# Idle products ahead of the data: 24 of 512 columns in place of 96 of 128 columns

## The chip, the cores and the metric

The kernel runs on one core of one Trainium2 chip. The metric is the device time of one execution in microseconds (us). The median of five executions of the kernel before is 330.3 us; they lie at 329.09, 329.21, 330.30, 330.36 and 330.72.

The engines are named as the profile names them: PE is TensorE's products and PEld its weight loads, DVE is VectorE, ACT is ScalarE, POOL is GpSimd, and SP is SyncE, whose queue (SPq) issues the transfers.

## The reference

Two stages follow each other: a retention layer in its parallel form, and a gated feed-forward layer.

```python
# q, k, v: 8 batches, 8 heads, 576 positions, 64 numbers a head, fp32
scores = (1 / sqrt(64)) * q @ k.T
gamma  = 1 - 2.0 ** (-5 - arange(8))              # one decay a head
ret    = (scores * where(i >= j, gamma ** (i - j), 0)) @ v
x      = ret.transpose(0, 2, 1, 3).reshape(4608, 512)
out    = (sigmoid(x @ w_gate) * (x @ w_val)) @ w_out   # 512 -> 1536 -> 512
```

## The kernel before

**The work.** The decay is split: k is multiplied by a table of falling powers and q by one of rising powers, so what is left of the mask is a triangle. The positions are taken in chunks of 128. The first 768 rows of x are made in a special way, as three pairs of chunks (`PAIRS`): a pair's k and q are cast to bf16 and scaled (`cast_pair`, L270), turned by TensorE with products against an identity (`pair_t`, L310, called through `turn`), copied out of PSUM by ScalarE (L320), multiplied to scores (`pair_qk`, L329), masked by VectorE (L334) and multiplied by v (`pair_intra`, L416). A state, the sum of k times v over earlier chunks, is kept beside (`pair_st`, L348, and `pair_inter`, L426). The other rows follow in steps (`slot`, `slot_of_two`), placed between the products of the feed-forward layer: gate and value products (`h_half` L881, `h_both` L802, `h_units` L698), sigmoid on ScalarE, product with the gate on VectorE, and the output product (`op_first` L952, `op_units` L765).

**The order.** It is written out by hand: each engine runs its instructions in the order in which the program names them. TensorE is one queue in order, so an instruction that waits holds all behind it. SyncE issues nearly all loads, in order, into a pool of 18 buffers (`ld`); a load waits until the buffer that it takes has been read. The weights are cast from fp32 to bf16 by GpSimd, ScalarE and VectorE (L244, L249).

**The idle products.** At the start there is nothing for TensorE to do until the first k and q are loaded and scaled. `blank` is a tile of 128 x 128 zeros, set by VectorE (L170). `idle_bank` (L174) takes a tile of 128 x 128 fp32 from the PSUM pool `ffn`, whose three buffers are a bank (512 fp32 a partition) each. `fill(n)` (L179) issues 4n products of blank by blank into it. Nobody reads the result. `fill(10)` comes right after `blank`; then the first pairs are worked on with more of it between:

```python
    cast_pair("q", 0, 0, nc.vector)
    turn("k", 0, 0, *TR)
    turn("q", 0, 0, *PV)
    fill(3)
    cast_pair("q", 0, 1, nc.vector)
    pair_qk(0, 0, QK)
    turn("k", 0, 1, *TR)
    fill(2)
    turn("q", 0, 1, *PV)
    fill(3)
    ...
```

and so on with `fill(2)`, `fill(1)` and, after a second `idle_bank()`, `fill(3)`: 24 units, 96 products (L182) in all, each with its own weight load.

Of the kernel before, what the change touches and what calls it, by code (L numbers as in the profile page):

```python
# [9 lines left out]
FP32 = mybir.dt.float32  # L10
# [6 lines left out]
def kernel(  # L17
# [19 lines left out]
    nc = tc.nc  # L37
# [4 lines left out]
    P = 128  # L42
# [18 lines left out]
    ffn_psum = ctx.enter_context(tc.tile_pool(name="ffn_psum", bufs=3, space=PS))  # L61
# [107 lines left out]
    blank = consts.tile([P, P], BF16)  # L169
    nc.vector.memset(blank, 0.0)  # L170

    idle = []

    def idle_bank():  # L174
        idle.append(ffn_psum.tile([P, P], FP32, tag="ffn", name=f"idle_{len(idle)}"))

    idle_bank()

    def fill(n):  # L179

        for i in range(4 * n):
            nc.tensor.matmul(idle[-1], lhsT=blank, rhs=blank, start=True, stop=True)  # L182

    fill(10)
    def tables(shape, pattern, step, put, fix=None):

# [643 lines left out]
# [9 lines that stand above are left out]
# [8 lines left out]
    fill(1)  # L847
    turn("q", 1, 1)
    idle_bank()
    fill(3)  # L850
    pair_intra(0, 0, 0)
# [221 lines left out]
```

## Time and profile before

| what | value |
| --- | --- |
| median of five executions | 330.3 us |
| the profiled execution | 329.21 us, of which the span (first to last instruction) is 327.5 us |
| TensorE busy | 321.3 us (98%), 3696 products |
| VectorE, ScalarE, GpSimd busy | 148.6, 139.1, 104.1 us |
| idle products (L182) | 96, 8.6 us of busy time, 1.05 to 13.3 us of the span |
| first gate product of the feed-forward layer (hg, L881) | 17.39 us |
| last product's modelled end | about 324.2 us |

How to read it: the profile shows one execution. A product's length in it runs to its modelled end, and products overlap, so how fast TensorE goes is seen from the distance between starts. "Idle before" is the time in which an engine did nothing, with what ended it. The chain of waits goes back from the last instruction to what released it, step by step, and so names what is on the path to the end.

### The profile page before, as it was taken

To read this page: it belongs to the slowest core of one execution; us is meant where nothing else is said; L and a number is where in the kernel's file an instruction comes from. 1 tells how busy PE (TensorE), PEld (TensorE's weight loads), DVE (VectorE), ACT (ScalarE), POOL (GpSimd) and SP (SyncE) were. 2 spreads that over 40 slices of the span, in tenths; PEclk is the share of its full clock that TensorE was granted. 3 is DMA by queue.
4 is the path that set the end of the run, shared out by engine and by line. 5 is a ranking of instruction groups with operands and counts; after the bars stand their busy time and mean duration, and the time that the engine had idled before them with its cause. 6 is when DMAs were issued, how large, how long until landed. Compare 5 with 4: busy or idle time off the path is not lost.

```text
span 327.5 us, 8910 instructions
## 1 busy us (share of the span) xinstructions
PE 321.3 (98%) x3696; PEld 173.0 (53%) x3696; DVE 148.6 (45%) x335; ACT 139.1 (42%) x314; POOL 104.1 (32%) x138
## 2 busy tenths in 40 slices
PE   8899999999999999999999999999999999999996
PEld 8774557856546554455444544454445544544443
DVE  6945756656505463445334534344444433404410
ACT  6654545554524354324532543335334533343321
POOL 5784637454535463018300840075003000000000
PEclk9999999999999999999999999999999999999999
DMA  7999999999996999809890799069805820010003
GB/s 209 352 396 384 377 242 213 202 177 218 206 196 143 215 219 200 187 2 199 199 247 2 151 229 254 15 124 214 210 2 73 304 109 2 34 74 27 1 32 98
DMA packets 144794, 55.16 MB, mean 168 GB/s; under 512 B 125168, under 2 KB 136688, under 8 KB 144752
## 3 DMA queue, kind: packets, MB, share of 16 engines
q1 hardware_dynamic: 144608, 54.44, 68.3%
q8 instruction: 29, 0.48, 0.6%
q10 hardware_dynamic: 144, 0.13, 0.1%
q14 instruction: 13, 0.11, 0.1%
HBM read 37.75 MB, written 9.44 MB: 144 GB/s over the span
## 4 chain that ended last, share of the span: by engine, by line
PE 97%; ACT 1%; DVE 1%; issue 0%; ACTq 0%
PE h L698 50%; PE op L765 25%; PE op L952 3%; PE hg L802 3%; PE hv L802 3%; PE val L509 2%; PE idle L182 2%; PE row L483 1%; PE row L491 1%; PE val L525 1%; PE op L754 1%; PE qkp L329 1%; ACT qT L320 1%; PE hv L881 1%; PE hg L881 1%; PE kTp L310 0%
## 5 line engine op out<-in xcount | busy, mean ns | idle before, releaser
L726 DVE TENSOR_TENSOR gv<-g,h 128x512 bf16<-128x512 bf16 (+1 forms) x96 | 62.8, 654 | 103.3 <-PE h L698 100.5
L698 PE MATMUL h<-xT,wv_sb 128*128 128x512 bf16 (+2 forms) x432 | 100.7, 356 | 0.0
L698 PE MATMUL h<-xT,wg_sb 128*128 128x512 bf16 (+2 forms) x432 | 100.7, 355 | 0.0
L722 ACT ACTIVATE g<-h 128x512 bf16<-128x512 f32 (+1 forms) x96 | 54.7, 570 | 94.4 <-PE h L698 90.9
L765 PE MATMUL op<-wo_sb,gv 128*128 128x512 bf16 x372 | 84.0, 379 | 0.0
L698 PEld LDWEIGHTS <-wg_sb 128*128 128x128 bf16 x432 | 42.0, 98 | 41.2
L698 PEld LDWEIGHTS <-wv_sb 128*128 128x128 bf16 x432 | 41.9, 98 | 40.4
L765 PEld LDWEIGHTS <-gv 128*128 128x128 bf16 x372 | 35.3, 98 | 41.0
L288 POOL CAST v<-v 128x512 bf16<-128x512 f32 x29 | 17.7, 610 | 89.4 <-PE val L509 80.1
L283 POOL TENSOR_TENSOR qk<-k,ktab 128x512 bf16<-128x512 f32 x30 | 31.3, 1042 | 33.4 <-DMA k<-in_k_dram 21.7
L741 ACT COPY ob<-op 128x512 f32<-128x512 f32 x33 | 19.3, 585 | 35.7 <-PE op L765 34.8
L283 POOL TENSOR_TENSOR qk<-q,qtab 128x512 bf16<-128x512 f32 x28 | 29.5, 1055 | 1.3 <-DMA q<-in_q_dram 1.0
L498 DVE TENSOR_TENSOR pt<-row,tri 128x256 bf16<-128x256 f32 x60 | 21.6, 416 | 13.9 <-PE row L491 12.4
L567 ACT CAST xT<-val 128x256 bf16<-128x256 f32 x46 | 15.0, 380 | 22.9 <-PE val L525 21.4
L610 DVE TENSOR_TENSOR s<-s,row 128x256 f32<-128x256 f32 x39 | 16.2, 416 | 1.3
L459 ACT CAST sb<-s 128x256 bf16<-128x256 f32 x44 | 15.9, 421 | 0.3 <-DVE s L610 0.2
L553 DVE COPY glance<-val 128x1 f32<-128x1 f32 x24 | 2.7, 154 | 23.4 <-PE val L525 22.7
L952 PE MATMUL op<-wo_sb,gv 128*128 128x512 bf16 x48 | 11.7, 380 | 0.0
L509 PEld LDWEIGHTS <-v 64*64 64x64 bf16 x480 | 6.2, 108 | 7.5 <-issue 7.5
L525 PE MATMUL val<-T,sb 64*64 64x64 bf16 x368 | 9.7, 195 | 0.3 <-DVE glance L553 0.3
L809 DVE TENSOR_TENSOR gv<-g,hv 128x512 bf16<-128x512 bf16 x10 | 6.7, 683 | 7.0 <-PE hv L802 7.0
L182 PE MATMUL idle<-blank 128*128 128x128 bf16 x96 | 8.6, 259 | 1.1 <-DVE blank L170 1.1
(102 smaller groups left out, 241.6 us busy)
## 6 DMA issues: line engine op xcount, KB each, us to landing
out_dram<-ob SPq DMA_DIRECT2D x31, 256.0 KB, 3.1
k<-in_k_dram SPq DMA_DIRECT2D x26, 256.0 KB, 3.8
q<-in_q_dram SPq DMA_DIRECT2D x26, 256.0 KB, 4.1
v<-in_v_dram SPq DMA_DIRECT2D x26, 256.0 KB, 4.5
wg<-in_moe_w_gate_dram SPq DMA_DIRECT2D x12, 256.0 KB, 5.1
wv<-in_moe_w_val_dram SPq DMA_DIRECT2D x12, 256.0 KB, 5.1
wo<-in_moe_w_out_dram SPq DMA_DIRECT2D x12, 256.0 KB, 4.9
k32p<-in_k_dram SPq DMA_DIRECT2D x6, 256.0 KB, 5.2
```

The lines of the kernel that those rows point to most:

```text
L283: eng.tensor_tensor(out=natural_qk[s][:, i].rearrange("p m (y d) -> p y m d", y=2), in0=by_halves(loaded[s][1 - i]), in1=tab, op=ALU.mult)
L288: eng(out=natural["v", s], in_=loaded[s][2])
L459: eng(out=state[key], in_=src)
L498: nc.vector.tensor_tensor(out=probs[s][:, y], in0=row_ps[s][y][:, 0], in1=tri.unsqueeze(1).to_broadcast([P, M, 64]), op=ALU.mult)
L610: nc.vector.tensor_tensor(out=new, in0=running[b], in1=p, op=ALU.add)
L698: nc.tensor.matmul(out, lhsT=w_sb[:, kc, fc * P:(fc + 1) * P], rhs=xT[:, kc, t0 + a:t0 + e], start=(kc == 0), stop=(kc == NKC - 1))
L722: nc.scalar.activation(out=g[:, 0:n], in_=h1[:, 0:n], func=AF.Sigmoid)
L726: nc.vector.tensor_tensor(out=gvs[some[0]][:, a:e], in0=g[:, 0:n], in1=h2[:, 0:n], op=ALU.mult)
L741: (eng or on_act)(out=ob, in_=opp)
L765: nc.tensor.matmul(opp, lhsT=gvs[fc][:, nb * P:(nb + 1) * P], rhs=wo_sb[:, fc, :], start=(fc == 0), stop=(fc == NFC - 1))
L802: nc.tensor.matmul(ps, lhsT=(wg_sb if what == "g" else wv_sb)[:, kc, fc * P:(fc + 1) * P], rhs=xT[:, kc, 0:4 * P], start=(kc == 0), stop=( ...
L952: nc.tensor.matmul(opps[nb], lhsT=gvs[fc][:, nb * P:(nb + 1) * P], rhs=wo_sb[:, fc, :], start=(fc == 0), stop=(fc == NFC - 1))
```

## The change

Each four products of 128 columns become one of 512. The moving operand is the same 128 x 128 zeros, read four times over through a broadcast in the middle dimension; the idle tile becomes as large as the bank. The units and their places stay, so 24 products and 24 weight loads are left of 96 and 96.

```diff
     def idle_bank():
-        idle.append(ffn_psum.tile([P, P], FP32, tag="ffn", name=f"idle_{len(idle)}"))
+        idle.append(ffn_psum.tile([P, 4, P], FP32, tag="ffn", name=f"idle_{len(idle)}"))
 
     idle_bank()
 
     def fill(n):
 
-        for i in range(4 * n):
-            nc.tensor.matmul(idle[-1], lhsT=blank, rhs=blank, start=True, stop=True)
+        for i in range(n):
+            nc.tensor.matmul(idle[-1], lhsT=blank, rhs=blank.unsqueeze(1).to_broadcast([P, 4, P]), start=True, stop=True)
 
     fill(10)
```

The instruction lists of the two programs differ on TensorE in these products and weight loads alone. On SyncE the order of the loads is the same, but three neighbouring pairs trade the buffers that they take: w_val's second and third piece for columns 8 to 11, w_out's first two rows of blocks, and k and q of step 1.

## Prediction

> **What bounds the kernel now.** I read the page first, then TensorE's waits, then the timeline and the chain of waits of the first 14 us, because the change touches nothing later.
>
> From the page: span, busy time of the first engine, and the granted clock.
>
> ```profile
> span 327.5 us, 8910 instructions
> ...
> PE 321.3 (98%) x3696; PEld 173.0 (53%) x3696; DVE 148.6 (45%) x335; ACT 139.1 (42%) x314; POOL 104.1 (32%) x138
> ...
> PEclk9999999999999999999999999999999999999999
> ```
>
> The reader is to see that TensorE is busy for 321.3 of 327.5 us, and the chain that ended last is 97% PE. Of the rest, about 3.3 us lie behind the last product, when the result is stored.
>
> All that TensorE waited for (waiter, releaser: total us, times, longest us):
>
> ```profile
> PE idle L182 <- DVE blank L170: 1.1, 1, 1.1
> PE qkp L329 <- ACT qT L320: 0.7, 3, 0.3
> PE st L348 <- ACT sbd L358: 0.7, 1, 0.7
> ```
>
> The first three rows, 2.5 us, lie in the first 16 us. From 16 us to the end only 0.5 us of waiting is left. So after the start TensorE is a queue without gaps: a delay or a gain that reaches 17.4 us, where the first gate product (hg, L881) starts, goes through to the end one to one. Everything rests on the first 17 us.
>
> TensorE's timeline there (start, length, line, what, count, idle before):
>
> ```profile
> 1.05 4.45 PE L182 MATMUL idle<-blank 128*128 128x128 bf16 x40 [1.05 <-DVE blank L170]
> 5.29 0.63 PE L310 MATMUL kTp<-ident,kp 128*128 128x128 bf16 x4
> 5.72 0.60 PE L310 MATMUL qTp<-ident,qp 128*128 128x128 bf16 x4
> 6.14 0.85 PE L182 MATMUL idle<-blank 128*128 128x128 bf16 x12
> 7.24 0.42 PE L329 MATMUL qkp<-qT,kT 64*64 64x128 bf16 x16 [0.24 <-ACT qT L320]
> 7.58 0.40 PE L310 MATMUL kTp<-ident,kp 128*128 128x128 bf16 x4
> 7.82 0.61 PE L182 MATMUL idle<-blank 128*128 128x128 bf16 x8
> 8.27 0.39 PE L310 MATMUL qTp<-ident,qp 128*128 128x128 bf16 x4
> 8.49 0.83 PE L182 MATMUL idle<-blank 128*128 128x128 bf16 x12
> 9.47 0.42 PE L329 MATMUL qkp<-qT,kT 64*64 64x128 bf16 x16 [0.15 <-ACT qT L320]
> ```
>
> A length here runs from the first start to the last modelled end, so I take spacing from starts. The first 40 idle products take 5.29 - 1.05 = 4.24 us to the next start, 106 ns each. The last 12 (8.49, length 0.83, one product 0.219 long) give (0.83 - 0.219) / 11 = 56 ns. The array thus ran at half rate until about 6.2 us, although the row of the granted clock shows 9 everywhere; the spacing is what I trust. One product of 128 columns is 315 ns long in the slow part and 219 in the fast one.
>
> The chain of waits (start, share in us, what) shows which of the idle products are on the path:
>
> ```profile
> 1.05 4.45 PE idle L182 x40
> 5.50 0.44 PE kTp L310 x4
> ...
> 7.98 0.45 PE idle L182 x8
> 8.43 0.24 PE qTp L310 x4
> ...
> 11.95 0.33 PE idle L182 x4
> ...
> 12.65 0.67 PE idle L182 x12
> ```
>
> So 64 of the 96 are on it; the other 32 fill time in which TensorE would wait for ScalarE's copy of qT anyway.
>
> **The change, part by part.**
>
> *Products.* 96 products and 96 weight loads become 24 and 24: 144 fewer instructions on TensorE (8910 to 8766). The columns stay 12,288. The instruction lists of the two programs show no other instruction of TensorE moved and no wait of it added.
>
> *The first ten.* No row shows a product of 512 columns at half rate. At full rate L802 gives it: 8 of them take 1.73 us in the chain of waits, 216 ns each, against 56 for 128 columns, a factor of 3.86. Bounds at half rate: 3.86 x 106 = 409 ns and 4 x 107 = 428 ns. Ten take 4.09 to 4.28 us, against 4.24. I take 4.24, because a rate of 1.2 columns per ns (128 / 107) leaves no fixed part to save. Even the lower bound gains only 0.15 us. More cannot be had here: kp, the next thing TensorE needs, is ready at 4.89 (GpSimd, 3.85 + 1.04), and qp at 5.44 (VectorE, 4.51 + 0.93), while qTp starts at 5.72.
>
> *The other fourteen.* At full rate 4 x 56 = 224 ns become 216, 8 ns less. On the path are 2 + 1 + 3 of them: 6 x 8 = 0.05 us. The other eight end earlier by 0.06 us in all, and TensorE then waits that much longer for qT (0.24 and 0.15 us now). The operand is blank read four times over; no row has such an operand on TensorE. The nearest rows are L802 (216) and four separate reads (224), so the cost lies between 0 and -0.05.
>
> *The bank.* The idle tile grows from 512 bytes a partition to the whole bank, in a pool whose other tiles are whole banks already. No reader waits for it, and the later writers are on the same engine: nothing.
>
> *Loads.* The order of SyncE's queue stays, but three neighbouring pairs of loads trade buffers, and so waits: wv of rows 1 and 2 for columns 8 to 11, wo 0 and 1, and k and q of step 1. The largest wait on that queue between 20 and 60 us is 2.9 us. The last of that wv is cast at 33.51 and TensorE wants it at 35.41 (slack 1.9); wo 1 is cast at 33.84 and wanted at 39.30 (5.5); q of step 1 is cast at 52.62 and turned at 56.51 (3.9). For the last pair the worst is that k's issue, which ends at 43.22, waits as long as q's now does, to 44.93: 1.7 us against 3.9. Cost nothing; without that cover it would be up to the excess over the slack.
>
> *Sum.* 0 (-0.15 to +0.04) for the first ten, -0.05 for the rest: about -0.1 us. The profiled execution took 329.21 us (span 327.5 and 1.7 around it), so it would become 329.1. But it is among the lower of five executions (329.09 to 330.72); from their median, 330.3, the forecast is **330.2**. Of this kernel about 0.3%, 1.0 us, can be told from no change.
>
> **A rule weighed against these rows.** The rows say 56 and 216 ns. The Trainium skill, "TensorE: Matmul & The Clock Gate", section "Back-to-back issue gap", states for streams of weight loads and products about 81 ns a product at 128 columns and 131 at 512. By it, an estimate, the idle work would fall from 96 x 81 = 7.8 us to 24 x 131 = 3.1, so the fill would no longer span the wait for data; by the rows it stays within 0.3 us of what it was. The rows decide. The same page, section "What's actually happening", says that the clock is released by time and not by a number of products, in windows that run free of the kernel's start; that supports equal releases, but no single trace can show it.
>
> **The rivals.**
>
> *Slower: the clock is released later.* For it: 106 ns turned into 56 only after 5.1 us of work, and if what is watched includes weight loads, the change takes away three in four. Against it: at half rate both forms keep the columns streaming without a gap. Price: one pass, from the qkp at 7.24 to that at 9.47, has 1.25 us of TensorE work on the path (7.24 to 8.49), which would double; and the 12 idle products behind it, 0.67 us now, would take 1.28 and outlast ScalarE's copy by some 0.4. So a release one pass later costs up to 1.65 us, and a release half a pass later 0.8: 331.1 to 331.95. It decides if the idle products of the second fill, from 6.1 us on, and those of the third still start about 400 ns apart. I give it 0.20.
>
> *Slower: code or loads late.* The 29 instruction packets of queue q8 take 0.6% of 16 x 327.5 us, 1.1 us each; each now falls 144 instructions later in the work. One that TensorE had to wait for would cost about 1.1 us: 331.3. Against it: TensorE waits for none of the 29 now. With the loads above, 0.05.
>
> *Faster: the release comes sooner.* The five executions lie at 329.09 and 329.21 and then at 330.30 to 330.72. If the time of the release separates them and wide products bring it forward each time, the median becomes that of the lower ones, 329.1. For it: nothing in the trace but the spread. Against it: an earlier release alone is worth little, because qp of the second half (VectorE, 7.24 + 0.69 = 7.93, held by its load) lets qTp start at most 0.3 us before its 8.27. I give it 0.18.
>
> **How the numbers follow.** No change within 0.3%: 0.57; slower 0.20 + 0.05 = 0.25; faster 0.18. The range runs from the faster case, with its 329.1 inside, to most of the later release: 329.0 to 331.8. The likeliest case alone: 329.7 to 330.7.
>
> **What would show it.** TensorE's timeline after: ten wide products from 1.05, about 427 ns apart, and kTp at 5.2 to 5.35; the qkp rows within 0.1 us of 7.24 and 9.47; hg (L881) at about 17.4; from there the same spacing, 216 ns for each product of 512 columns. The forecast is wrong if the wide products start 216 ns apart early, if qkp moves by over 0.5 us, if TensorE gets a wait for issue, or if k of step 1 makes turn wait at 56.5.

## The result and the profile after

The changed kernel takes 330.21 us (median of 38 executions, 329.14 to 333.63), the kernel before 329.46 (66 executions, 328.95 to 330.72). The ratio is 1.003, with a 95% interval of 1.002 to 1.0039: **slower by 0.3%**, 0.75 us between the medians. The five executions that the prediction started from, with a median of 330.3, had by chance drawn the kernel before too high by 0.84 us.

The spread has changed more than the middle. Of the 38 executions six lie above 331.5, three of them at 333.3 to 333.6; of the 66 before none lies above 330.8.

The page of the changed kernel, and what its TensorE waited for (waiter, releaser: total us, times, longest):

```profile
span 328.1 us, 8766 instructions
...
q8 instruction: 28, 0.46, 0.6%
```

```profile
PE st L348 <- ACT sbd L358: 0.7, 1, 0.7
PE qkp L329 <- ACT qT L320: 0.5, 3, 0.2
PE st L348 <- issue: 0.4, 1, 0.4
...
PE kTp L310 <- POOL kp L270: 0.2, 1, 0.2
```

Two rows are new. One is a short wait for kp. The other is a stop of TensorE in L348 that nothing in the profile releases: "issue" means that the engine waited for no semaphore that is seen.

The timeline of TensorE after the change:

```profile
1.05 4.12 PE L182 MATMUL idle<-blank 128*128 128x512 bf16 x10 [1.05 <-DVE blank L170]
5.01 0.39 PE L310 MATMUL kTp<-ident,kp 128*128 128x128 bf16 x4
...
6.72 0.42 PE L329 MATMUL qkp<-qT,kT 64*64 64x128 bf16 x16 [0.17 <-ACT qT L320]
7.39 0.40 PE L310 MATMUL kTp<-ident,kp 128*128 128x128 bf16 x4 [0.25 <-POOL kp L270]
...
9.44 0.42 PE L329 MATMUL qkp<-qT,kT 64*64 64x128 bf16 x16 [0.18 <-ACT qT L320]
...
16.17 0.35 PE L348 MATMUL st<-vp,kp 64*64 64x64 bf16 x11
16.96 0.25 PE L348 MATMUL st<-vp,kp 64*64 64x64 bf16 x5 [0.44 <-issue]
...
17.81 0.61 PE L881 MATMUL hg<-xT,wg_sb 128*128 128x256 bf16 x4
```

The same sixteen products of L348 in the kernel before, in one piece:

```profile
16.35 0.44 PE L348 MATMUL st<-vp,kp 64*64 64x64 bf16 x16
```

The reader is to see three things. The wide products start as forecast, about 427 ns apart, but the array changed to its full rate sooner in this execution, so qkp starts 0.5 us earlier (6.72 against 7.24); most of that is given back in the wait for kp. At 16.2 us TensorE is still 0.2 us ahead. Then the sixteen products, which have no wait in their instructions, break after the eleventh. From the start of the eleventh to that of the twelfth 0.63 us pass, where there were 0.03, and hg comes at 17.81 instead of 17.39, 0.42 late. The two spans differ by 0.6 us; the last 0.14 gathers in small pieces after 100 us and was not followed.

**What stops it.** TensorE's code comes in packets of 16 KB on queue q8: 29 before, for 7392 products and weight loads, and 28 after, for 7248. That makes a packet about 256 instructions. I call the place where one packet's instructions end and the next one's begin a border. In the changed kernel's trace the stop stands between TensorE's 449th and 450th instruction. In the stretch before it, one such packet travels among the loads:

```profile
q1 hardware_dynamic: 758, 0.73, 104.5%
q8 instruction: 1, 0.02, 2.7%
```

That is the view of the transfers from 14 to 16 us: 16 engines fully taken by loads, and one code packet. The trace's transfer records have it from 14.71 to 15.59 us. TensorE stops at 16.32 and goes on at 16.96, 1.37 us after the packet's end. In the kernel before, that packet lands at 11.02, and TensorE reaches its 449th instruction at 13.98. The change took 144 instructions out ahead of this point, so the border moved to a later place in the work. There the packet has less time, for two reasons. It starts 3.0 us after TensorE has reached the border before (its 193rd instruction, at 11.69), where in the kernel before it starts 1.5 us after (8.60). And TensorE, with many short products, goes from the one border to the next in 4.6 us in place of 5.4.

### The profile page after: what moved, and what is told of

It is laid out like the page before. It is cut to its first block, busy times and chain, and to the rows that moved or that the text cites. A ratio compares the mean times of both kernels' runs of the same rounds, so it can differ in the third digit from the quotient of the medians.

```text
span 328.1 us, 8766 instructions
## 1 busy us (share of the span) xinstructions
PE 321.2 (98%) x3624; PEld 167.9 (51%) x3624; DVE 148.5 (45%) x335; ACT 139.2 (42%) x314; POOL 104.8 (32%) x138
## 3 DMA queue, kind: packets, MB, share of 16 engines
HBM read 37.75 MB, written 9.44 MB: 144 GB/s over the span
## 4 chain that ended last, share of the span: by engine, by line
PE 95%; DMA 1%; ACT 1%; DVE 1%; issue 0%; POOL 0%; SPq 0%; ACTq 0%
PE h L698 50%; PE op L765 25%; PE op L952 3%; PE hv L802 3%; PE hg L802 3%; PE val L509 2%; PE row L483 1%; PE row L491 1%; DMA k32p<-in_k_dram 1%; PE val L525 1%; PE op L754 1%; PE hv L881 1%; PE hg L881 1%; PE qkp L329 1%; PE st L348 1%; PE idle L182 0%
## 5 line engine op out<-in xcount | busy, mean ns | idle before, releaser
L610 DVE TENSOR_TENSOR s<-s,row 128x256 f32<-128x256 f32 x39 | 16.2, 416 | 1.3
L483 PE MATMUL row<-T 64*64 64x64 bf16 x480 | 9.7, 197 | 0.0
```

Of the source, the lines that this page charges most:

```text
L610: nc.vector.tensor_tensor(out=new, in0=running[b], in1=p, op=ALU.add)
```

## The experiments

Theory 1 is the one just given: the code is late, and only where the border lies matters. Theory 2 is the rival that I had held likelier: the width of the products, or the fewer weight loads, cost something through the clock or the array. All kernels compute the whole output.

For the reading of all of them: the interval of a ratio is 95%, and the kernel before took 329.41 us (35 executions) beside the first four and 329.29 (23 executions) beside the others.

**Narrow products, and more instructions.**

```diff
-    fill(10)
+    def fill_small(n, w):
+
+        for i in range(n):
+            nc.tensor.matmul(idle[-1][0:w, 0:w], lhsT=blank[:, 0:w], rhs=blank[:, 0:w], start=True, stop=True)
+
+    fill_small(96, 53)
```

> As the kernel before, but the first fill is 96 products of 53 columns in place of 40 of 128: the same 4.24 us, and 112 more instructions, where the change has 144 fewer. Code comes in packets of 256 instructions, so 112 more put the packet borders where 144 fewer put them. Theory 1 (code late): TensorE stops for 'issue' in st L348 at about 16.5 us, as after the change, 0.2 to 1 us; time 0.2 to 0.5% over before, with single executions above 331. Theory 2 (width: fewer weight loads or wide products cost, through the clock or the array): all products are narrow and weight loads are more than before, so no stop, and the time of before within 0.1%.

Measured: 330.14 us (329.08 to 332.27), ratio 1.0031 (1.0015 to 1.0048). The whole loss of the change is there with narrow products and more weight loads than before. The profile fell on the shortest execution, and even that shows the stop (this kernel's lines are 5 further on, so L348 is L353):

```profile
16.13 0.58 PE L353 MATMUL st<-vp,kp 64*64 64x64 bf16 x16
```

0.58 us in place of 0.44. The view of waits doesn't list this stop, because the modelled lengths of the products cover it; the starts show it. It stands behind the 705th instruction of TensorE: 449 + 256, the next border, at the same place in the work. The packet ended at 15.17, and TensorE went on at 16.46, 1.29 us later. Theory 2 fails here as the cause of the loss.

**Wide products, and as many instructions as before.** The later 14 units stay wide; the first fill is in small pieces.

```diff
-    fill(10)
...
+    fill_small(82, 62)
```

> As the changed kernel, with its 14 later wide products, but the first fill is 82 products of 62 columns (4.24 us), so that TensorE has as many instructions as before the change ahead of each real one. Theory 1 (code late): no stop for issue at 16.5 us, and the time of before or up to 0.2 us below it. Theory 2 (width of the later products): slower by 0.2 to 0.4%, as after the change.

Measured: 329.43 us (328.98 to 330.02), ratio 1.0001 (0.9989 to 1.0013), and no stop in L348. The fourteen wide products cost nothing that can be measured. As it has 82 products in its first fill, it doesn't speak for the ten wide ones there; the kernel of half width, further on, does for 256 columns.

This trace has a stop all the same, one border later, behind the 705th instruction, which here stands at the same place in the work as in the kernel before. The same eight products in the kernel before and here (L886 is L881, 5 lines further on):

```profile
19.41 1.04 PE L881 MATMUL hg<-xT,wg_sb 128*128 128x256 bf16 x8
```

```profile
19.49 1.18 PE L886 MATMUL hg<-xT,wg_sb 128*128 128x256 bf16 x8
```

Between the 705th and the 706th instruction 0.25 us pass, where there are 0.11 in the kernel before. The packet ended at 19.01, and TensorE went on at 20.40, 1.38 us later. So a border can be short of time in a kernel that hasn't fewer instructions, too; here it cost the traced execution 0.14 us.

**First fill narrow, the rest wide.** 84 instructions fewer.

```diff
-    fill(10)
+    def fill_narrow(n):
+
+        for i in range(4 * n):
+            nc.tensor.matmul(idle[-1][:, 0, :], lhsT=blank, rhs=blank, start=True, stop=True)
+
+    fill_narrow(10)
```

> The first fill as before (40 narrow products), the other 14 units wide: 84 instructions fewer than before. Theory 1 (code late): between two borders of 256 instructions TensorE needs 5.0 us there, against 3.9 us with 144 fewer and 5.3 before, so no stop or a rare one: within 0.1% of before. Theory 2 (fewer weight loads after the first fill): at least half of the change's 0.3%. If what matters is the number of instructions taken away, 84 of 144 of it, 0.17%.

Measured: 329.37 us (328.87 to 329.69), ratio 1.0001 (0.9992 to 1.0009), no stop. More than half of the 144 instructions are gone without a cost that can be measured.

**The changed kernel once more.**

> The changed kernel itself, beside the others on one chip, for a second trace. Theory 1 (code late): again a stop for issue at the eleventh to twelfth product of st L348 at 16.3 to 16.5 us; its length is what differs between executions, so the traced execution's time over 329.2 is about the stop less 0.2. Theory 2: the first difference to before lies elsewhere, at the release of the clock.

Measured: 330.06 us (329.38 to 332.01), ratio 1.0024 (1.0012 to 1.0035). The profiled execution took 330.06 us too, and has the stop at the same instruction, longer:

```profile
16.28 0.35 PE L348 MATMUL st<-vp,kp 64*64 64x64 bf16 x11
17.26 0.25 PE L348 MATMUL st<-vp,kp 64*64 64x64 bf16 x5 [0.63 <-issue]
```

0.82 us from start to start, against 0.63 in the first trace, and a span of 328.3 us against 328.1: the 0.2 us by which the two differ. The expectation, 329.2 plus the stop less 0.2, gives 329.8; it was 330.06.

**Half the width.** 48 products of 256 columns, 96 instructions fewer.

```diff
-        for i in range(n):
-            nc.tensor.matmul(idle[-1], lhsT=blank, rhs=blank.unsqueeze(1).to_broadcast([P, 4, P]), start=True, stop=True)
+        for i in range(2 * n):
+            nc.tensor.matmul(idle[-1][:, 0:2], lhsT=blank, rhs=blank.unsqueeze(1).to_broadcast([P, 2, P]), start=True, stop=True)
```

> 48 idle products of 256 columns: 96 instructions fewer than before, at the same length of time. Theory 1 (code late): on the undisturbed times of the kernel before, TensorE passes the 256 instructions ahead of the second border in 4.5 us, against 3.9 with 144 fewer and 5.0 with 84 fewer, so the stop is there only when the packet is late by more than usual: 0 to 0.15% over before, an occasional execution above 331, and where there is a stop, it is in front of the instruction 48 later than in the changed kernel. A theory by which each instruction taken away costs the same gives two thirds of the change, 0.2%.

Measured: 329.17 us (328.56 to 329.54), ratio 0.9983 (0.9962 to 1.0005), no stop in the trace and no execution above 329.6. The median lies a little below what theory 1 allowed (0 to 0.15% over before), the interval reaches into it, and there were no late executions at all. Two thirds of the 144 instructions are gone, and none of the loss is there; the 0.2% of a cost for each instruction taken away lies outside the interval. Here all idle products, those of the first fill too, are wider than before.

**The loads held back.** The changed kernel; SyncE stops behind its twelfth load until the first state is written, and the weights are loaded and cast later.

```diff
-    load_w(0, 2)
-    load_w(2, 2)
...
     tile_sv(0, 0, (on_act, on_act))
+    gate_sb = consts.tile([64, M, 64], BF16)
+    nc.sync.dma_start(out=gate_sb, in_=sbd[0][half(0), :, half(0)])
+    load_w(0, 2)
+    load_w(2, 2)
...
```

> The changed kernel, with SyncE's queue held after the first twelve loads until the first state is written (about 14.5 us); the weights come some 6 us later, so the time is above before by several us and says nothing. The question is the first code packet of TensorE. If it is late because it waits behind loads on the transfer engines, it starts at 12 to 13.5 us in place of 14.7 to 14.9, and TensorE doesn't stop in front of st L348's twelfth product (apart from waits for weights). If its delay has nothing to do with loads, it starts at 14.2 to 14.9 and the stop of 0.2 to 0.8 us stays.

Measured: one execution, 335.87 us, as it has to wait for its weights. The transfers from 12 to 16 us, in the changed kernel first and then in this one (stretch, length, busy time of the engines with counts, granted clock, DMA share, GB/s):

```profile
12.00:14.00 2.00, 2.00 (x68) 1.39 (x70) 1.49 (x3) 0.75 (x1) 1.80 (x4) 1.00 1.06 355
14.00:16.00 2.00, 1.33 (x56) 1.09 (x48) 1.93 (x4) 1.35 (x4) 1.85 (x4) 1.00 1.07 372
```

```profile
12.00:14.00 2.00, 2.00 (x67) 1.36 (x68) 1.49 (x3) 0.74 (x1) 1.67 (x4) 1.00 0.30 91
14.00:16.00 2.00, 1.33 (x57) 1.08 (x49) 1.92 (x4) 1.31 (x4) 0.39 (x1) 1.00 0.03 6
```

TensorE's part (the first number behind the length) is the same in both, and it reaches the border before, its 193rd instruction, at 11.72 here and at 11.69 there. What differs is the transfers, 1.06 of the engines' time against 0.30, and GpSimd, which has no weights to cast. The packet now starts at 13.06 us, where it started at 14.71 and 14.91, and L348 (L338 here) runs through:

```profile
16.21 0.44 PE L338 MATMUL st<-vp,kp 64*64 64x64 bf16 x16
```

So without the loads the packet came 1.7 to 1.9 us sooner, and the stop was gone. This is one execution, and when TensorE asks for a packet isn't recorded. The other packets of the nine traces agree, though. For each I take the time from TensorE's reaching the border before to the packet's start, and the share of the engines that the loads had taken in the 1.5 us ahead of that start. With the engines free (share under 0.05), none of 65 packets started later than 1.50 us. With them full (over 0.9), 58 of 145 did, up to 4.49 us. Late packets go with loads.

This kernel begins exactly as the changed one does, and shows by chance the other thing: its array was still at half rate in kTp (0.63 us for four, against 0.39 in the changed kernel's first trace), and its first fill took as long as that of the kernel before.

```profile
1.05 4.45 PE L172 MATMUL idle<-blank 128*128 128x512 bf16 x10 [1.05 <-DVE blank L160]
5.29 0.63 PE L300 MATMUL kTp<-ident,kp 128*128 128x128 bf16 x4
```

The moment at which the array changes its rate thus differs between executions that start alike, and in the nine traces it doesn't go with the width.

**The kernel before, without its second fill.** A try at a better one.

```diff
     turn("k", 0, 1, *TR)
-    fill(2)
     turn("q", 0, 1, *PV)
```

> The kernel before with narrow products, without the first fill(2) (8 products) ahead of the turning of q's second half, where the chain of waits has 0.45 us of it and the data are ready 0.3 us earlier; 16 instructions fewer. If those products are on the path: 0.2 to 0.3 us less than before (0.06 to 0.1%). If VectorE or the loads bound that pass: no difference. Theory 1 (code late): 256 instructions in 5.0 us there, so no stop.

Measured: 329.25 us (328.85 to 329.4), ratio 0.9981 (0.9959 to 1.0002); between the medians 0.04 us. In its trace the time goes into a wait:

```profile
8.23 0.40 PE L310 MATMUL qTp<-ident,qp 128*128 128x128 bf16 x4 [0.57 <-DVE qp L270]
```

TensorE waits for VectorE where it made idle products before, and qTp starts at 8.23 against 8.27. What the chain of waits had as 0.45 us of idle products was a cover over a wait for data. Neither this kernel nor the one of half width is faster than before by more than the measurement can tell.

**All traces together.** From the transfer records and the starts of TensorE's instructions: when the packet behind the border that matters (the second packet of the queue for the kernel with 112 more instructions, the first for the others) has landed, when TensorE reaches the border, and the stop. The stop is the distance between the two starts at the border; where there is none, it is 0.03 or less, and 0.11 in the row of the next border. Times in us.

```
kernel                    landed  border reached  between  stop
before                     11.02          13.98     2.96   none
changed                    15.59          16.32     0.73   0.63
changed, second trace      15.86          16.43     0.58   0.82
112 more, narrow           15.17          16.28     1.12   0.17
as many as before           9.02          14.06     5.04   none
  its next border          19.01          20.14     1.13   0.25
84 fewer                   13.11          15.60     2.49   none
96 fewer, half width       13.55          15.77     2.22   none
changed, loads held        13.93          16.36     2.43   none
16 fewer, no second fill   12.38          13.91     1.53   none
```

Where there was a stop, TensorE went on 1.29 to 1.40 us after the packet's end; where 1.53 us or more lay between, there was none. One rule covers all ten rows. At every other border of the nine traces 2.0 us or more lay between.

## Why the prediction was wrong

- **The first ten products.** Right in size. Behind the first, they start 426 to 427 ns apart until the array changes its rate. kTp started at 5.01 and not between 5.2 and 5.35, because the array changed its rate 1.4 us sooner than in the trace of before; the loads held gave 5.29.
- **The other fourteen.** Right: 215 to 216 ns apart. The 0.05 us is too little to be told in any time measured here. The read of the zeros through a broadcast has no price of its own: 216 ns is also what L802 takes.
- **The bank and the loads that trade buffers.** Right: no wait of TensorE after the change answers to them; turn (L444) sits idle for none of its products.
- **"An earlier release alone is worth little."** Right, and shown: in the first trace qkp came 0.5 us earlier and lost 0.3 of it to kp and the rest to the next fill and qp; the second qkp started at 9.44 against 9.47.
- **A delay at 17.4 us "goes through to the end one to one".** Nearly right for the stop: 0.42 us late at hg and 0.56 at the last products, 0.72 and 0.84 in the second trace. A small lead can be lost on the way: in the trace with the first fill narrow, hg came 0.33 us earlier than before, and the last products 0.03 later. Where it went was not followed.
- **The rival of the later release**, at 0.20, was wrong. Narrow products lost as much as wide ones, and wide ones without the shifted border lost nothing.
- **The step that failed** is the one on code: "TensorE waits for none of the 29 now", and for that reason 0.05. The mechanism stood there as a rival, with a price of 1.1 us, and in the sum it stood at nothing. The changed kernel's two traces show 0.63 and 0.82 from start to start, and its median is 0.75 higher. What I did not do is to put the new border into the old trace. There TensorE passes the 256 instructions ahead of it in 3.9 us (4.6 and 4.8 in the changed kernel itself, where fewer of them are idle products and they reach further back), against 5.4 at the old place, and in a stretch where the loads take all transfer engines. That no packet is late now says nothing of a border moved by 144 instructions, if the margin at the new place has not been worked out. Each border had a margin in that trace, 2.0 us or more between the packet's end and TensorE. In the changed kernel's first trace one has 0.73, and all others have 3.6 or more. Of the signs of being wrong that the prediction named, two came: a wait for issue, and qkp moved by 0.52 us, the second through the array's earlier change of rate.
- **The number.** 330.2 against 330.21 is luck: the base was 0.84 us too high, and the 0.75 us of the loss were not in it. From the true median the same sum gives 329.4. A slight gain was forecast; there is a loss, and the interval of 0.2 to 0.39% excludes no change.

What stays open is what lengthens the executions above 331.5; none of them was traced. Their mean granted clock was 0.989 to 0.995, against 0.998 to 1.0 in all others but one (331.07, with 0.993). The trace with the loads held shows what such a clock stands for. After two waits of 1.9 us for weights its clock record stands at half from 20.2 to 27.1 us, and its mean clock is 0.990 (the third number from the end is the granted clock):

```profile
20.00:22.00 2.00, 0.51 (x3) 0.39 (x4) 0.00 (x0) 0.00 (x0) 1.15 (x2) 0.56 0.97 288
22.00:24.00 2.00, 2.00 (x26) 1.40 (x25) 0.42 (x1) 1.15 (x4) 1.31 (x3) 0.50 1.07 369
```

An estimate: the share of the clock that is missing, times the span, is what such a stretch costs. Without it the six lie at 329.7 to 330.8, among the others; the one of 331.07 comes to 328.8, a little below them. So the six most likely had a stretch at half rate; that a longer stop for code set it off is only argued. Beside the last three kernels the kernel before, too, had one execution of 333.3 with a clock of 0.988, which comes to 329.3 that way, so it isn't safe from it.

## What to carry to other kernels

Instructions taken out or put in move every later border between code packets; here a packet is 256 instructions of TensorE. Before you call such an edit neutral, shift the borders in the old trace by that number, and look for stretches in which small products run fast while loads fill the transfer engines: in these traces TensorE needed its packet landed some 1.4 us before it got there. Such a loss shows as a wait for "issue" amid instructions without waits, and in a wider spread of the times. A short stop shows in the distances between starts alone. The stop of the changed kernel went away with 48 or 60 more idle instructions ahead of it.

## What the runs showed of the hardware

- A code packet of 16 KB took 0.88 to 0.95 us on its queue at the borders of the table, and after a stop TensorE went on 1.29 to 1.40 us after its end.
- With the transfer engines taken (share 1.06 to 1.07) the packet started 1.7 to 1.9 us later than with them nearly free (0.30, one execution). Over all traces no packet started later than 1.50 us after TensorE had reached the border before when the engines were free, and 58 of 145 did when they were full.
- The array changed from 107 to 56 ns for 128 columns at 4.5 to 6.9 us of the span (narrow first fills 4.8 to 6.9, wide ones 4.7 to 6.6, half width 4.5), with no relation to the width of the products that a trace would show, while the profile's row of the granted clock stood at full throughout.
- After two waits of 1.91 and 1.88 us the array ran at half rate from 20.2 to 27.1 us (loads held), and there the row of the granted clock shows it.
